# Attention and two GLU layers on one core: two small loads moved to ScalarE's queue, merged output stores, another accumulator bank

## The chip, the cores and the metric

The kernel runs on one core of one Trainium2 chip. The metric is the device time of one execution in microseconds (us); the time of a version is the median of its runs. One core has five engines that run side by side and wait for each other through semaphores: TensorE (PE; weight loads are PEld), VectorE (DVE), ScalarE (ACT), GpSimd (POOL) and SyncE (SP). Sixteen DMA engines move data between HBM and the on-chip memories. An engine starts a transfer by an issue instruction in its own queue; SP does nothing else.

## The reference

Inputs are q, k and v of shape (4 batches, 8 heads, 576 tokens, 64) in float32, a matrix omega (128 x 64) and six weight matrices. Per head, `phi(x) = exp(h - max h) / sqrt(m)` with `h = x_s omega^T - |x_s|^2 / 2`, where `x_s` is x scaled by 64^(-1/4). Then `kv = phi(k)^T v`, `z = sum of phi(k)`, and the result is `phi(q) kv / (phi(q) z + 1e-6)`. The heads are put side by side, giving 2304 rows of 512, and two GLU layers follow: `(silu(x Wg) * (x Wv)) Wo`, and the same with a sigmoid and other weights. The widths are 512, 1536 and 512. The output is 2304 x 512 in float32.

## The kernel before

**Attention.** It is worked off in 16 pairs of heads. A batch's 576 tokens are 512 main tokens and 64 last tokens. The main tokens of q and k are loaded by `Pair.load` (line 340) as 128 partitions of four tokens; the last tokens go to a tile `kqrem` of 128 partitions by 64 elements, where partition and row together stand for head and token. For the first pair alone (line 343) that is one transfer of 32 KB for k and one for q; their DRAM side is `src[0, :2, MAIN:, :]`, two stretches of memory of 64 rows each, one of either head. For other pairs a transfer per head is used (line 348). A list ORDER, written by hand, says which step of which pair stands after which in every engine's program. For the first pair ScalarE's order is: square of k (`mk`, line 379), square of the last tokens (`mr`, line 379), upper half of the transposed k (`hi_k`, line 406), square of q (`mq`). TensorE's order is: 14 idle transposes at the start, transposes of k (`tp_k`), of the last tokens (`tp_r`), products of k with omega (`pj`, line 420), transposes of q (`tp_q`), further products, and much later the products with v (`kv`, line 480). So `mr` and `tp_r` stand in front of everything else of the pair, and both read `kqrem`.

**Layers.** The 2304 rows are worked off in three sets of 768. The first layer of the first set runs beside the making of the weights; the other five passes (layer and set) use a Strassen form of the two first products, in which tiles X, Y, Z of PSUM (two banks each; X has two tiles in turn, Y and Z one each) take sums of products, and ScalarE and VectorE read them in `gate` and `total`. `gate` reads the first bank by an ACT instruction and the second by a DVE instruction (line 875) that stands a step later in the program. Behind each pass stands the third product: twelve slices, each with 18 matmuls into six accumulators, which are the two banks of Y, of Z and of one X tile (`acc`, line 981). In the three passes of the second layer the six accumulators b = 0..5 are copied to SBUF, by VectorE for even b and by ScalarE for odd b (lines 1007 to 1010), into four tiles used in turn (`u2`, `p5`, `s0`, `s2`, so b = 4 takes the tile of b = 0, and b = 5 that of b = 1). Each copy is stored to `out` from SP's queue by `store` (line 202); 128 main tokens of one batch take one transfer of 256 KB. In the very last pass (third set, `ahead is None`) the copies 2 and 5 are the last tokens of all four batches, 32 rows of each, and take four transfers of 64 KB, so SP issues twelve there.

Of the kernel before, what the change touches and what calls it, by code (L numbers as in the profile page):

```python
# [32 lines left out]
def tile_performer_attention__then__two_glu_layers(  # L33
# [25 lines left out]
    nc = tc.nc  # L59
    P = 128  # L60
    B, H, S, D = q.shape
# [3 lines left out]
    MAIN = NB * P  # L65
# [42 lines left out]
    class Weight:  # L108
# [11 lines left out]
        def load(self):  # L120
            l, c, n = self.key
            fs = slice(c * P, (c + 1) * P)
            w = weights[l][n]
            view = w[fs, :] if n == 2 else w[:, fs].rearrange("(k p) f -> p k f", p=P)
            if l == 0:
                self.res = wres.tile([P, KC * P], F32, tag=f"w{n}_{c}", name=f"w{n}_{c}")
                wf[self.key] = self.res
            if not self.cast:
                self.place()
                nc.sync.dma_start(  # L130
                    out=self.res if n == 2 else self.res.rearrange("p (k f) -> p k f", k=KC),
                    in_=view,
                )
                return
            raw64 = self.raw = wraw.tile([P, KC * P, 2], U32, name="raw64")
            nc.sync.dma_start(
                out=raw64.rearrange("p f w -> p (f w)")
                if n == 2
                else raw64.rearrange("p (k f) w -> p k (f w)", k=KC),
                in_=view.bitcast(U32),  # L140
            )
            self.lo, self.hi = raw64[:, :, 0], raw64[:, :, 1]
# [58 lines left out]
    def store(o, i):  # L201
        nc.sync.dma_start(out=o, in_=i)
# [69 lines left out]
    with ExitStack() as st:  # L272
# [47 lines left out]
        class Pair:  # L320
# [10 lines left out]
            def load(self):  # L331
                b, h0 = self.b, 2 * self.hp
                self.v = vbuf[self.n % len(vbuf)]
                if self.hp == 0:
                    rems[b] = spare(2 + b % 2, [P, NP, 2, D], name="kqrem"), vrbuf[b % len(vrbuf)]
                self.r, self.vr = [x[:, self.hp] for x in rems[b]]
                main = lambda x: x[b, h0:h0 + 2, :MAIN, :].rearrange("h (p i) d -> p h i d", i=NB)
                for n, name, src in (0, "k", k), (1, "q", q):
                    t = raw.tile([P, 2, NB, D], F32, name=name + "raw")
                    nc.sync.dma_start(out=t, in_=main(src))  # L340
                    setattr(self, name, t)
                    if self.n == 0:
                        nc.sync.dma_start(out=self.r[:, n, :], in_=src[0, :2, MAIN:, :])
                if self.n == 1 or self.hp == 0 and self.n > 0:
                    for n, src in (0, k), (1, q):
                        for h, hs in enumerate(halves):
                            tail = src[b, h::2, MAIN:, :].rearrange("n p d -> p n d")
                            nc.sync.dma_start(
                                out=rems[b][0][hs, self.hp:, n, :], in_=tail[:, self.hp:]
                            )  # L350
# [425 lines left out]
    with tc.manual_schedule():  # L776
# [3 lines left out]
        acc = [ps_a.tile([P, MAIN], F32, tag=f"acc{j}", name="acc") for j in range(6)]  # L780
        late = pool("late", 1, side="right")
        for c in range(FC):
# [11 lines left out]
            ahead = [of_w(0, c + 1, n) for n in range(2)] if c + 1 < FC and not w_next else []  # L794
            w2 = of_w(0, c, 2)
            assert {(0, c, 2)} | {(0, c + 1, n) for n in range(2) if ahead} <= done, c
            p, n = jobs[c]
# [16 lines left out]
            t = wsum.tile([P, 4, H2], F32, tag="s", name="wsums")  # L814
# [33 lines left out]
        ps_yz, ps_x = pool("ps_yz", 1, space=PSUM), pool("ps_x", 2, space=PSUM)  # L848
        tmp, hall = pool("tmp", 1), pool("hall", 1)
        bank = lambda p, tag: p.tile([P, 2, MAIN], F32, tag=tag, name=tag)  # L850
# [12 lines left out]
        rows = out.rearrange("(b s) e -> b s e", s=S)  # L863
# [69 lines left out]
        for at, (layer, n) in enumerate(STRASSEN):  # L933
            h, hs = {}, {}
            ahead = STRASSEN[at + 1][1] if at + 1 < len(STRASSEN) else None
            for p in range(FC // 2):
                X, Y, Z = bank(ps_x, "X"), bank(ps_yz, "Y"), bank(ps_yz, "Z")
                u2, p5 = [tmp.tile([P, 2, TS], F32, tag=x, name=x) for x in ("u2", "p5")]
                for c in (2 * p, 2 * p + 1):
                    h[c] = h_tile(c)  # L940
                h1, h2 = [[h[c][:, ab] for ab in range(2)] for c in (2 * p, 2 * p + 1)]
                for k in range(7):
                    dst = (X, Z, X, Y, X, Z, X)[k]
                    w = ready.pop(o)
                    for i in range(2):
                        for kk in range(2):
                            fs = slice(i * H2 + kk * P, i * H2 + (kk + 1) * P)
                            l, r = [u[:, fs] for u in w], xc[k, kk]
                            for j, (a, b) in enumerate(((0, 0), (0, 1), (1, 0))):
                                nc.tensor.matmul(  # L950
                                    dst[:, i, :TS],
                                    lhsT=l[a],
                                    rhs=r[b],
                                    start=k in (0, 1) and kk == 0 and j == 0,
                                    stop=kk == 1 and j == 2,
                                    skip_group_check=True,
                                )
                    if k == 0:
                        copy(both(Y), X)
                    if k == 1:  # L960
                        copy(p5, Z)
                    if k == 2:
                        copy(u2, X)
                    if k == 3:
                        after(1, partial(gate, layer, h1[0], both(Y)))
                    if k == 4:
                        total(layer, h2[1], X, p5)
                    if k == 5:
                        total(layer, h1[1], Z, u2)
                    if k == 6:  # L970
                        after(1, partial(gate, layer, h2[0], both(X)))
                    clock += 1
                    run()
                    prepare(o + AHEAD)
                    o += 1
                    for _ in range(1 + (k == 0)):
                        next(making, None)
                    if p == FC // 2 - 1 and k in (3, 5):
                        c = (k - 3) // 2
                        hs[c] = h_split(c)  # L980
            acc = [bank(ps_yz, "Y"), bank(ps_yz, "Z"), bank(ps_x, "X")]
            acc = [t[:, i, :] for t in acc for i in range(2)]
            for c in range(FC):
                w, now = ready.pop(o), hs.pop(c)
                if layer == 0:
                    second(acc, now, w, c == 0, c == FC - 1)
                else:
                    for b in range(6):
                        js = slice(b % 3 * P, (b % 3 + 1) * P)
                        l = [u[:, b // 3, js] for u in now]  # L990
                        three(acc[b], l, w, c == 0, c == FC - 1)
                clock += 2
                run()
                if c + 2 < FC:
                    hs[c + 2] = h_split(c + 2)
                prepare(o + AHEAD)
                o += 1
                for _ in range(2):
                    next(making, None)
                if ahead is not None:  # L1000
                    x_parts(ahead, c)
            for b in range(6):
                if layer == 0:
                    result(acc, n, LAST[b])
                    continue
                t = tmp.tile([P, DM], F32, tag=("u2", "p5", "s0", "s2")[b % 4], name="o")
                if b % 2:
                    nc.scalar.activation(t, acc[b], AF.Copy)
                else:
                    nc.vector.tensor_copy(t, acc[b])  # L1010
                q, ab = 3 * n + b % 3, b // 3
                batch = q // 2
                if batch < B:
                    i = 2 * (q % 2) + ab
                    dst = rows[batch, :MAIN, :].rearrange("(p i) e -> i p e", i=NB)[i]
                    store(dst, t)
                    continue
                for batch in range(B):
                    half = REM // 2
                    dst = rows[batch, MAIN + ab * half:MAIN + (ab + 1) * half, :]  # L1020
                    store(dst, t[batch * half:(batch + 1) * half])
        assert next(making, "none") == "none"


# [32 lines left out]
```

## Time and profile before

| what | value |
|---|---|
| median of 3 runs | 1054.29 us (1053.64 to 1056.53) |
| the profiled execution | 1055.49 us |
| its span, first to last instruction | 1053.7 us |
| PE busy | 1019.9 us, 97% of the span |
| DVE, ACT busy | 71%, 57% |
| DMA queue of SP | 49.5% of sixteen engines' span |

The profile shows one execution. Busy shares are means over stages with different limits: over the span the matmul engine is hardly ever idle, and its few idle stretches lie at the start and behind the last matmul, with some in the middle where weights are made. The granted clock of TensorE has two levels, 1.2 and 2.4 GHz, shown as 0.5 and 1.0. A timeline row gives start, duration, engine, line and tiles, and in brackets how long the engine had been idle and what released it. A row of the windows gives a stretch, its length, then for PE, PEld, DVE, ACT and POOL the busy time and in brackets the instructions that started, the granted clock, the share of the DMA engines and GB/s.

### The profile page before, as it was taken

The numbers are of one execution on the slowest core, as the hardware profiler recorded it, in microseconds if no ns is written. First come the engines' busy times: TensorE is split into PE (matmuls) and PEld (weight loads), VectorE is DVE, ScalarE is ACT, GpSimd is POOL, SyncE is SP. The second block draws the span as 40 slices with busy tenths as digits, with TensorE's granted clock in tenths as the row PEclk, the third lists the DMA queues.
The fourth block names the chain that finished last, engine by engine and source line by source line (L and its number), as shares of the span: only waits on it lengthen the run. The fifth ranks groups of instructions, "written<-read, shape, count | busy, mean of one in ns | idle before, by whom it ended". The sixth has DMA issues, their size and how long they took to land.

```text
span 1053.7 us, 17289 instructions
## 1 busy us (share of the span) xinstructions
PE 1019.9 (97%) x6079; PEld 956.8 (91%) x6079; DVE 752.0 (71%) x1526; ACT 595.7 (57%) x1259; POOL 86.4 (8%) x110
## 2 busy tenths in 40 slices
PE   8999999889999999999999999999999999999997
PEld 7999999889889989989899889898899998999985
DVE  6899996759785677887777886877655565556642
ACT  6999996324333655545555455655555554555532
POOL 2111112111110000000000000011000000000000
PEclk8999999999999999999999999999999999999999
DMA  7443422599794677756788666888244442444421
GB/s 204 137 127 111 107 81 81 157 238 258 215 263 142 172 221 225 213 163 179 199 239 251 172 178 197 259 245 214 81 150 131 130 114 67 141 130 125 117 79 61
DMA packets 138156, 173.15 MB, mean 164 GB/s; under 512 B 32852, under 2 KB 87124, under 8 KB 138068
## 3 DMA queue, kind: packets, MB, share of 16 engines
q1 hardware_dynamic: 129140, 155.78, 49.5%
q0 software_dynamic: 8928, 16.26, 8.6%
q8 instruction: 48, 0.79, 0.3%
q14 instruction: 40, 0.33, 0.1%
HBM read 122.72 MB, written 33.03 MB: 148 GB/s over the span
## 4 chain that ended last, share of the span: by engine, by line
PE 65%; DMA 11%; DVE 10%; issue 7%; ACT 4%; SPq 1%; POOL 0%; ACTq 0%; DVEq 0%; POOLq 0%
PE X L950 13%; PE Z L950 7%; DMA wp<-wf 6%; PE pj L420 4%; PE Y L950 4%; PE X L735 3%; PE Y L735 3%; PE kv L480 3%; PE Z L735 3%; ACT vh L238 3%; PE o L506 2%; DVE vl L242 2%; DMA raw<-in_moe_w_gate_dram 2%; PE acc L735 2%; DMA w<-mag 2%
## 5 line engine op out<-in xcount | busy, mean ns | idle before, releaser
L242 DVE TENSOR_TENSOR vl<-wp,vh 128x512 fp32r<-128x512 f32 x270 | 186.1, 689 | 147.6 <-ACT vh L238 147.3
L238 ACT ACTIVATE vh<-wp 128x512 fp32r<-128x512 f32 x270 | 167.5, 620 | 30.3 <-DMA wp<-wf 26.9
L950 PE MATMUL X<-xhi,vh 128*128 128x384 f32 x480 | 161.4, 336 | 5.6 <-DVE p L891 3.5
L950 PE MATMUL X<-xhi,vl 128*128 128x384 f32 x480 | 160.6, 335 | 0.1
L950 PE MATMUL X<-xlo,vh 128*128 128x384 f32 x480 | 160.4, 334 | 0.0
L882 ACT ACTIVATE hh<-h 128x768 fp32r<-128x768 f32 x60 | 50.6, 844 | 107.2 <-PE X L261 67.4
L883 DVE TENSOR_TENSOR hl<-h,hh 128x768 fp32r<-128x768 f32 x60 | 57.5, 958 | 64.9 <-ACT hh L882 64.7
L950 PEld LDWEIGHTS X<-xhi,vh 128*128 128x128 f32 x480 | 90.1, 188 | 8.9 <-issue 5.6
L950 PEld LDWEIGHTS X<-xhi,vl 128*128 128x128 f32 x480 | 90.1, 188 | 0.4 <-DVE vl L242 0.4
L950 PEld LDWEIGHTS X<-xlo,vh 128*128 128x128 f32 x480 | 90.1, 188 | 0.2
L950 PE MATMUL Z<-xhi,vh 128*128 128x384 f32 x240 | 81.4, 339 | 3.1 <-ACT vh L238 1.9
L950 PE MATMUL Z<-xhi,vl 128*128 128x384 f32 x240 | 81.5, 340 | 0.9
L950 PE MATMUL Z<-xlo,vh 128*128 128x384 f32 x240 | 80.3, 335 | 0.0
L151 ACT ACTIVATE mag<-raw 128x512 f32<-128x512 f32 x72 | 48.3, 673 | 38.5 <-DMA w<-mag 18.8
L260 PE MATMUL pg<-xhi,whi 128*128 128x384 f32 x160 | 56.1, 351 | 11.4 <-ACT s L806 11.4
L183 POOL DMA_DIRECT2D res<-mag x36 | 31.1, 864 | 385.2 <-DVE mag L177 370.1
L262 PE MATMUL pg<-xhi,wlo 128*128 128x384 f32 x160 | 55.5, 347 | 0.0
L261 PE MATMUL pg<-xlo,whi 128*128 128x384 f32 x160 | 55.5, 347 | 0.0
L950 PEld LDWEIGHTS Z<-xhi,vh 128*128 128x128 f32 x240 | 45.1, 188 | 6.0 <-ACT vh L238 4.2
L874 ACT ACTIVATE g<-p 128x384 f32<-128x384 f32 x30 | 15.8, 526 | 61.3 <-DVE p L891 61.3
L950 PEld LDWEIGHTS Z<-xhi,vl 128*128 128x128 f32 x240 | 45.0, 188 | 4.3 <-DVE vl L242 4.1
L177 DVE SCALAR_TENSOR_TENSOR mag<-raw,mag 128x512 f32<-128x512 uint32 x72 | 48.1, 687 | 0.8
(208 smaller groups left out, 2680.0 us busy)
## 6 DMA issues: line engine op xcount, KB each, us to landing
wp<-wf SPq DMA_DIRECT2D x210, 256.0 KB, 2.8
wp<-ws SPq DMA_DIRECT2D x60, 256.0 KB, 2.7
raw<-in_moe_w_gate_dram SPq DMA_DIRECT2D x24, 512.0 KB, 4.3
raw<-in_moe_w_val_dram SPq DMA_DIRECT2D x24, 512.0 KB, 4.4
raw<-in_moe_w_out_dram SPq DMA_DIRECT2D x24, 512.0 KB, 5.2
wf<-wsums SPq DMA_DIRECT2D x48, 256.0 KB, 4.8
res<-mag POOLq DMA_DIRECT2D x36, 256.0 KB, 5.2
w<-mag POOLq DMA_DIRECT2D x26, 256.0 KB, 8.6
```

The source lines that it names most:

```text
L151: nc.scalar.activation(self.mag, self.hi.bitcast(F32), AF.Abs, scale=REBIAS)
L177: nc.vector.scalar_tensor_tensor(self.mag, self.lo, 2.0**-52, self.mag, ALU.mult, ALU.mult)
L238: nc.scalar.activation(self.parts[0], self.src, AF.Copy)
L242: self.eng.tensor_tensor(lo, self.src, hi.bitcast(F32), ALU.subtract)
L260: nc.tensor.matmul(o, lhsT=l[0], rhs=r[0], start=start, stop=False)
L261: nc.tensor.matmul(o, lhsT=l[0], rhs=r[1], start=False, stop=False)
L262: nc.tensor.matmul(o, lhsT=l[1], rhs=r[0], start=False, stop=stop)
L420: nc.tensor.matmul(out_ap, lhsT=l[:, i, :], rhs=r, start=n == 0, stop=n == 2)
L735: nc.tensor.matmul(o, lhsT=l[a], rhs=r[b], start=start and i == 0 and not (tail and j % 2), stop=stop and i == 2, skip_group_check=tail,)
L882: nc.scalar.activation(hi, h[c], AF.Copy)
L883: nc.vector.tensor_tensor(lo, h[c], hi.bitcast(F32), ALU.subtract)
L950: nc.tensor.matmul(dst[:, i, :TS], lhsT=l[a], rhs=r[b], start=k in (0, 1) and kk == 0 and j == 0, stop=kk == 1 and j == 2, skip_group_chec ...
```

## The change

Three things are changed. The two loads of the first pair's last tokens are issued by ScalarE and not by SP. In the copies of the second layer's three passes ScalarE takes b = 0 and 1, VectorE takes 2 to 5; the last tokens of all four batches go out in one transfer of 256 KB instead of four, so six transfers are left at the end; in the very last pass the stores of b = 2 and b = 4 are issued by ScalarE. In the very last pass a second X tile is allocated, and the sixth accumulator is its first bank and no longer the second bank of the first X tile.

```diff
                     if self.n == 0:
-                        nc.sync.dma_start(out=self.r[:, n, :], in_=src[0, :2, MAIN:, :])
+                        nc.scalar.dma_start(out=self.r[:, n, :], in_=src[0, :2, MAIN:, :])
...
             acc = [bank(ps_yz, "Y"), bank(ps_yz, "Z"), bank(ps_x, "X")]
+            if ahead is None:
+                acc.append(bank(ps_x, "X"))
             acc = [t[:, i, :] for t in acc for i in range(2)]
+            if ahead is None:
+                acc[5:] = acc[6:7]
...
-                if b % 2:
+                if b // 2 == 0:
                     nc.scalar.activation(t, acc[b], AF.Copy)
                 else:
                     nc.vector.tensor_copy(t, acc[b])
                 q, ab = 3 * n + b % 3, b // 3
                 batch = q // 2
+                queue = nc.scalar if ahead is None and b in (2, 4) else nc.sync
                 if batch < B:
                     i = 2 * (q % 2) + ab
                     dst = rows[batch, :MAIN, :].rearrange("(p i) e -> i p e", i=NB)[i]
-                    store(dst, t)
-                    continue
-                for batch in range(B):
+                    queue.dma_start(out=dst, in_=t)
+                else:
                     half = REM // 2
-                    dst = rows[batch, MAIN + ab * half:MAIN + (ab + 1) * half, :]
-                    store(dst, t[batch * half:(batch + 1) * half])
+                    dst = rows[:, MAIN + ab * half:MAIN + (ab + 1) * half, :]
+                    queue.dma_start(out=dst, in_=t)
```

## Rows read from the trace of the kernel before

**Rows 1.** The page: busy time, share of the span, instructions.
```profile
PE 1019.9 (97%) x6079; PEld 956.8 (91%) x6079; DVE 752.0 (71%) x1526; ACT 595.7 (57%) x1259; POOL 86.4 (8%) x110
```
**Rows 2.** Chain of waits, 0 to 40 us: start, duration, what.
```profile
2.90 4.61 DMA kqrem<-in_q_dram
...
10.39 0.85 PE tp_q L400 x4
11.24 1.29 PE pj L420 x6
...
18.58 0.77 PE pj L420 x6
19.35 0.44 PE tp_q L400 x4
```
**Rows 3.** Timeline of ScalarE, 0 to 17 us.
```profile
0.75 1.28 ACT L379 ACT_TABLE_LOAD   x1 [0.75 <-PEq L1041]
...
7.81 0.58 ACT L406 ACTIVATE hi_k<-tp_k 128x512 fp32r<-128x512 f32 x1
```
**Rows 4.** Timeline of TensorE, the first 17 us.
```profile
4.86 0.60 PE L400 MATMUL tp_k<-ident,kraw 128*128 128x128 f32 x4
...
16.46 0.39 PE L480 MATMUL kv<-vr,fk 128*128 128x130 f32 x2
```
**Rows 5.** Windows of the start: busy time by engine, clock, DMA.
```profile
4.63:8.05 3.42, 1.13 (x8) 0.73 (x7) 1.29 (x4) 0.46 (x2) 0.86 (x3) 1.00 0.81 226
8.05:14.87 6.82, 6.42 (x27) 5.80 (x28) 4.43 (x13) 3.77 (x12) 1.42 (x2) 0.50 0.97 245
```
**Rows 6.** Timeline of the copies at the end, 1030 to 1054 us.
```profile
1044.14 0.69 DVE L1010 COPY o<-Y 128x512 f32<-128x512 f32 x1 [3.83 <-PE Y L262]
...
1045.50 0.69 DVE L1010 COPY o<-Z 128x512 f32<-128x512 f32 x1 [0.67 <-PE Z L262]
...
1047.11 0.69 DVE L1010 COPY o<-X 128x512 f32<-128x512 f32 x1 [0.92 <-DMA out_dram<-o]
1047.88 0.60 ACT L1008 ACTIVATE o<-X 128x512 f32<-128x512 f32 x1 [1.06 <-DVE o L1010]
```
**Rows 7.** Chain of waits, 1044 to 1054 us.
```profile
1044.86 2.13 DMA out_dram<-o
```
**Rows 8.** SP's last issue, and the landing of the last three issues.
```profile
1050.66 0.42 SPq L202 DMA_DIRECT2D out_dram<-o  x1
...
out_dram<-o SPq DMA_DIRECT2D x3, 64.0 KB, 2.0
```
**Rows 9.** Timeline of SP's queue, 0 to 8 us.
```profile
1.68 0.70 SPq L343 DMA_DIRECT2D kqrem<-in_k_dram  x1
...
2.90 0.57 SPq L343 DMA_DIRECT2D kqrem<-in_q_dram  x1
```
**Rows 10.** DMA issues, 0.7 to 0.8 and 10.1 to 10.2 us: KB, us to landing.
```profile
om<-in_omega_dram SPq DMA_DIRECT2D x1, 32.0 KB, 1.9
...
vr<-in_v_dram SPq DMA_DIRECT2D x1, 64.0 KB, 3.6
```
**Rows 11.** DMA packets from 3.55 to 4.00 us, then from 4.00 to 4.45.
```profile
DMA packets 104, 0.06 MB, mean 136 GB/s; under 512 B 58, under 2 KB 104, under 8 KB 104
...
DMA packets 103, 0.08 MB, mean 180 GB/s; under 512 B 32, under 2 KB 103, under 8 KB 103
```
**Rows 12.** Window of the last two passes.
```profile
800.00:1030.00 230.00, 230.00 (x1218) 215.96 (x1217) 132.60 (x200) 117.86 (x203) 0.00 (x0) 1.00 0.40 112
```
**Rows 13.** DMA from 1045.6 to 1047.2 us: packets, and the share of sixteen engines.
```profile
DMA packets 302, 0.56 MB, mean 347 GB/s; under 512 B 31, under 2 KB 31, under 8 KB 302
...
q1 hardware_dynamic: 302, 0.56, 95.2%
```
**Rows 14.** Timelines around the first slice of the last third product.
```profile
1001.10 0.39 PE L260 MATMUL X<-vh,hh 128*128 128x512 f32 x1
...
1001.82 0.55 DVE L875 TENSOR_TENSOR h<-g,X 128x384 f32<-128x384 f32 x1
```

## Prediction, before the result was known

> **What bounds the kernel now.** I read the page first: TensorE is busy for 97% of the span [rows 1], so over most of it only TensorE's own work counts, and I look for what the change moves at the two ends, where TensorE stands still. Next the chain of waits over the first 40 us: from 2.90 to 7.51 us it consists of one load, the second of the first pair's two small ones [rows 2]. ScalarE's square of the last tokens needs that load, and `hi_k`, from which all products of the pair follow, stands behind the square in program order: it starts at 7.81 [rows 3], although its own input, the transposed k, was ready at 5.46 [rows 4]. The windows show what this costs further on: the granted clock, 1.0 up to 8.05 us, is 0.5 from there to 14.87, behind a stretch in which TensorE was busy for 1.13 of 3.42 us [rows 5]. Last I read the end: the copies run one after the other, and VectorE and ScalarE take turns on the two banks of one PSUM tile; the chain goes through the store of the first copy, whose SBUF tile the fifth needs again [rows 6, 7]; SP's twelfth issue starts at 1050.66 and its data land about 2.0 us later [rows 8], at 1052.66, some 1.0 us ahead of the span's end.
>
> **The change part by part.**
>
> *The two small loads.* They leave SP's queue, where they took 0.70 + 0.57 us [rows 9], so every load behind them can be issued about 1.3 us sooner. On ScalarE they have cover: nothing but the load of the function table runs there until k has landed. If they are issued ahead of that table load, the second is issued near 1.5 us, else near 2.8 (0.75 + 1.28 + 0.70) [rows 3, 9]. How soon do they land? The omega load, just as large at 32 KB, needs 1.9 us when it is alone [rows 10]; the small load needed 4.61 [rows 2]. Two things make the difference: it stands behind 256 KB transfers in one queue, and it does not use all DMA engines. From 4.00 to 4.45 us, 32 packets of under 512 B (only the small loads have such) make 18 GB/s, about what one engine moves; from 3.55 to 4.00 us 58 make 33 GB/s, about two [rows 11]. So 32 KB take 1.0 us at that rate, two loads 2.0, and sharing the engines with k and q some more. Issued at 0.75 and 1.5 us, the second should land between 4.4 and 5.2 us; then ScalarE waits for it no longer, and `hi_k` starts when the transposes end, at 5.5 in place of 7.81: **-2.3 us**. Bounds: at best that (the transposes come late next); at worst, with the table load ahead and landing near 6.5, -0.9.
>
> *The clock.* Starting the products at 6.1 instead of 8.4 closes most of the idle stretch ahead of 8.05 us, so the clock may stay at its upper level. What half the clock costs: a group of six products takes 1.29 us at half and 0.77 at full clock, four transposes 0.85 and 0.44 [rows 2]. Up to ScalarE's next wait there are two such groups and one set of transposes: 2 x 0.52 + 0.41 = 1.45 us. Behind it ScalarE and VectorE are nearly as long as TensorE, and TensorE at full clock has new holes, in which the clock may fall later. Bounds -1.5 and +0.5; I take **-1.0**, nearer to the full price, since the cause of the fall goes. What is late next are v and its last tokens for `kv`, at 16.46 us [rows 4] less 3.3, that is 13.2; the last of these loads is issued at 10.12 and lands 3.6 us later [rows 10], 1.3 us sooner after the change: 12.4. That is a cover of 0.8 us.
>
> *The copies at the end.* ScalarE copies both banks of Y from 1044.14 on, 0.60 us each; VectorE both of Z from 1045.50 on, 0.69 each; so the turn-taking between engines goes. The fifth copy still waits for the first store: issue near 1044.76 plus 2.13 gives 1046.9, so it runs from 1047.0 to 1047.7, the sixth to 1048.4, as before (1048.48) [rows 6, 7]. No gain there. The stores on ScalarE stand behind its last copy and delay nothing. In the two passes before, the same turn-taking goes, and the next pass's tiles come free sooner; TensorE has no idle time there to give back (230.00 of 230 us busy [rows 12]): 0, either way.
>
> *The merged stores.* Six SP issues fewer: the last store starts at 1048.4 in place of 1050.66. With all sixteen engines it would land 2.13 us later, at 1050.6: -2.0 us, the lower bound. But the merged store has the form of the small load: one side 128 partitions, the other a few separate stretches of memory, here four. Two stretches kept about two engines busy, so I expect four here.
> The Trainium skill ("DMA: Bandwidth & Descriptors", section "Why a DMA increments its semaphore by 16 and not by 1") says that a transfer is spread over the largest number of engines, up to 16, which divides the slowest dimension of both its sides; for the small load that is 2 and for the merged store 4. By that rule the sum comes out as I take it, by its absence as in the first rival; the rates above agree with 2.
> An engine moves 347 / 0.952 / 16 = 22.8 GB/s with packets of 2 KB [rows 13]. Each of the four has to move 64 KB of b = 2, 64 KB of b = 5 and 16 KB each of b = 3 and 4, that is 164 kB, or 7.2 us. Work begins with the store issued at 1046.2; 256 KB at 347 GB/s are 0.75 of the 2.13 us, so 1.4 is what a transfer needs besides. 1046.2 + 1.4 + 7.2 = 1054.8 against 1052.66: +2.1 us. If the two merged stores went to different engines, b = 5 alone would land at 1048.4 + 1.4 + 2.9 = 1052.7: 0.0. I take **+2.1**: that the small load needed 2.7 us more than omega while its data need 1.0 says that it queues behind others on its own engines.
>
> *The sixth accumulator.* Its copy no longer shares a tile with the fifth; both stand on VectorE, so nothing comes of it. It costs where it is allocated: the second X tile is still being read when the first slice wants it. VectorE reads it from 1001.82 to 1002.37; the slice's sixth group would start at 1001.10 [rows 14]. That read is the other bank and later in the program, so I take **0**; if the whole tile has to be free, TensorE waits 1.3 us. Below zero nothing is to be had, as TensorE has no gap there [rows 12].
>
> **Sum.** -2.3 - 1.0 + 2.1 + 0 = -1.2 us; the profiled execution's 1055.49 becomes 1054.3. That execution lies 1.2 above the median of the runs shown, so for the median 1054.29 I expect 1053.1 us. What this kernel's measurements can tell from no change is about 0.3%, 3.2 us, so this is no visible change. The likeliest case's own range is 1050.3 (a whole clock gain, no queueing: -2.3 - 1.5 + 0) to 1056.5 (-0.9 + 2.1 + 1.3, less or more).
>
> **Rivals.**
>
> *The merged store uses all engines.* For it: every other store of the end does, at 347 GB/s. Against it: the small load, of the same form, does not. Tail -2.0, head -3.3: 1054.29 - 5.3 = 1049.0 us, faster.
>
> *The loads gain only their issue time.* The engines, and not the queue, hold the load: k and q still share its two engines. For it: in 4.00 to 4.45 us the small packets get one engine's rate while larger ones flow. Against it: the wait of 2.7 us is mostly its place in the queue. Then the second load is issued at 1.5 instead of 2.90: -1.4, the clock falls as before, and the end costs +2.1: 1055.0 us, slower than before, though not visibly; with the table load ahead -0.1 and 1056.3. It decides where the second load lands later than 7.5 - 2.1 = 5.4 us.
> The Trainium skill states this ("DMA: Bandwidth & Descriptors", section "Issuing engines are not separate DMA queues"): transfers issued from several engines run on the same sixteen DMA engines and interleave, and issuing from several saves issue time alone.
>
> *The merged store uses fewer than four engines.* With two, each has 2 x 128 + 2 x 16 = 288 KB, 295 kB or 12.9 us of work, and the last data land at 1060.5: +7.8, in sum +4.5, 1058.8 us, slower. It outweighs the head as soon as an engine's work passes 8.4 us. For it only that I know no store of this form in the trace; against it that two stretches had two engines.
>
> **How the numbers follow.** Forecast 0.53, all engines 0.20, issue time alone 0.20, fewer than four 0.07. Faster by over 0.3% (under 1051.1 us): nearly all of the first rival, 0.18, and the forecast's lower end, 0.12: 0.30. Slower by over 0.3% (above 1057.5): 0.06 of the third rival and 0.01 of the second: 0.07. Within: 0.63. The range is 1048.6 to 1056.0: it takes in most of the first rival and of the second, and leaves out the third and the outer ends.
>
> **What would show it.** In the changed kernel's chain of waits the small load is gone from the first 8 us, `hi_k` starts near 5.5 us, and the window from 8.05 us on shows a clock of 1.0 for most of its length. At the end there are six stores, the last issued near 1048.4 less the head's gain, and the two merged ones take over 4 us to land, the last one longest, with DMA rates near 90 GB/s. TensorE has no idle time at the first slice of the last third product. I am wrong if the merged store lands within 2.5 us (then 1049), if `hi_k` still waits for the small load, or if the head's gain is lost before the layers begin.

## The result and the profile after

The changed kernel takes 1061.73 us in the median of 6 runs (1059.77 to 1063.78), the kernel before 1053.97 (6 runs): a ratio of 1.0068, interval 1.0048 to 1.0088. It is slower by about 7.2 us (5.1 to 9.3). The forecast was 1053.1 us and no visible change, with a range up to 1056.0.

The page of the changed kernel, its first two lines: the span grew by 8.3 us, from 1053.7 to 1062.0, TensorE's busy time by 3.5, from 1019.9 to 1023.4 [rows 1].

```profile
span 1062.0 us, 17296 instructions
...
PE 1023.4 (96%) x6079; PEld 958.3 (90%) x6079; DVE 753.7 (71%) x1529; ACT 594.4 (56%) x1256; POOL 86.9 (8%) x110
```

**The start.** The chain of waits of the changed kernel, 0 to 40 us (start, duration, what): the small load is still what everything waits for, and it takes 5.30 us where it took 4.61 [rows 2]. Six products still take 1.29 us.

```profile
0.75 1.16 ACTq L343
...
1.94 5.30 DMA kqrem<-in_q_dram
...
10.13 0.85 PE tp_q L400 x4
10.98 1.29 PE pj L420 x6
...
18.32 0.77 PE pj L420 x6
```

ScalarE's timeline in the changed kernel: both loads are issued ahead of the table load, as the forecast hoped, and still `hi_k` starts at 7.55 and not at 5.5 [rows 3].

```profile
2.51 1.28 ACT L379 ACT_TABLE_LOAD   x1 [2.51 <-issue]
...
7.33 0.31 ACT L379 ACTIVATE mr<-kqrem 128x128 f32<-128x128 f32 x1 [2.25 <-DMA kqrem<-in_q_dram]
7.55 0.58 ACT L406 ACTIVATE hi_k<-tp_k 128x512 fp32r<-128x512 f32 x1
```

**The last third product.** TensorE's and VectorE's timelines of the changed kernel in its first slice, then the window of the last two passes: one wait of 1.24 us, released by VectorE's read of the old X tile, and 228.76 us of work where there were 230.00 [rows 12, 14]. Matmuls overlap, so the idle time is less than the delay: from the start of the matmul ahead of the wait to that of the thirteenth behind it the kernel before needs 2.94 us (1000.88 to 1003.82), the changed one 4.45 (1002.37 to 1006.82), which is 1.5 us more.

```profile
1003.31 0.55 DVE L875 TENSOR_TENSOR h<-g,X 128x384 f32<-128x384 f32 x1
```
```profile
1004.00 0.47 PE L260 MATMUL X<-vh,hh 128*128 128x512 f32 x1 [1.24 <-DVE h L875]
```
```profile
800.00:1030.00 230.00, 228.76 (x1214) 214.89 (x1213) 132.91 (x200) 116.52 (x202) 0.00 (x0) 1.00 0.40 113
```

**The end.** The timeline of the changed kernel from 1045.5 us on: the copies keep their order, as worked out, and the last of six stores is issued at 1051.40, 1.6 us behind the last matmul (1049.43 + 0.39).

```profile
1047.14 1.09 ACT L1012 ACTIVATE o<-Y 128x512 f32<-128x512 f32 x2 [4.82 <-PE Y L262]
...
1048.50 1.29 DVE L1014 COPY o<-Z 128x512 f32<-128x512 f32 x2 [5.19 <-PE Z L262]
...
1049.22 0.64 ACTq L1025 DMA_DIRECT2D out_dram<-o  x1
1049.43 0.39 PE L262 MATMUL X<-vh,hl 128*128 128x512 f32 x1
1050.02 1.35 DVE L1014 COPY o<-X 128x512 f32<-128x512 f32 x2 [0.23 <-DMA out_dram<-o]
1050.74 0.35 ACTq L1021 DMA_DIRECT2D out_dram<-o  x1
1051.40 0.69 SPq L1025 DMA_DIRECT2D out_dram<-o  x1
```

DMA of the changed kernel from 1047 to 1061 us, in 40 slices of 0.35 us (share of the sixteen engines in tenths, and GB/s): full rate of up to 392 GB/s for the first two stores, then a stretch in which several stores share the engines, then a plateau at two to three tenths, some 80 GB/s, that runs out at 1059.9. In the kernel before the engines moved 347 GB/s in the mean with its stores [rows 13].

```profile
DMA  0000399950578696665332222222222221100000
GB/s 0 0 0 0 140 386 375 392 205 0 123 228 222 222 334 176 140 152 111 64 88 76 88 64 64 70 76 82 99 88 82 82 94 53 59 29 29 0 0 0
```

From the last matmul to the end of the span the kernel before needs 6.9 us, the changed one 12.2. So of the profiles' 8.3 us, 5.3 lie behind the last matmul, 1.5 are the wait, and the start gives 0.3 back; the other 1.8 lie in the middle, where of the change there are only the copies of the two earlier passes of the second layer (see what stays open).

### The profile page after: what moved, and what is told of

It is laid out like the page before. It is cut to its first block, busy times and chain, and to the rows that moved or that the text cites. A ratio compares the mean times of both kernels' runs of the same rounds, so it can differ in the third digit from the quotient of the medians.

```text
span 1062.0 us, 17296 instructions
## 1 busy us (share of the span) xinstructions
PE 1023.4 (96%) x6079; PEld 958.3 (90%) x6079; DVE 753.7 (71%) x1529; ACT 594.4 (56%) x1256; POOL 86.9 (8%) x110
## 4 chain that ended last, share of the span: by engine, by line
PE 68%; DVE 10%; DMA 10%; issue 6%; ACT 4%; POOL 0%; SPq 0%; ACTq 0%; DVEq 0%; POOLq 0%
PE X L950 14%; PE Z L950 7%; DMA wp<-wf 5%; PE Y L950 4%; PE pj L420 4%; DMA raw<-in_moe_w_gate_dram 3%; PE X L735 3%; PE Y L735 3%; PE kv L480 3%; PE Z L735 3%; PE o L506 2%; PE acc L735 2%; DVE vl L242 2%; ACT vh L238 2%; PE pg L260 2%
```

## The experiments

Each kernel was profiled, and those with an interval were timed against the kernel before on the same chip. "The end" is the span less the end of the last matmul, from one execution of each; the kernels of the table ran on several chips, so ratios are compared and not times:

```
kernel            span    last matmul ends   the end   ratio to before (interval)
before            1053.7   1046.83             6.9     -
changed           1062.0   1049.82            12.2     1.0068 (1.0048 to 1.0088)
merged_only       1057.0   1045.55            11.5     1.0047 (1.0032 to 1.0062)
acc_only          1052.8   1045.92             6.9     1.0029 (1.0013 to 1.0044)
head_only         1052.1   1045.25             6.9     1.0016 (1.0003 to 1.0030)
copies_only       1052.4   1045.64             6.8     1.0007 (0.9995 to 1.0019)
spread_only       1050.1   1044.54             5.6     0.9979 (0.9963 to 0.9996)
spread_all        1054.6   1048.97             5.6     1.0018 (1.0000 to 1.0035)
head_four         1054.8   1047.98             6.8     0.9991 (0.9971 to 1.0011)
best_mix          1048.9   1043.45             5.5     0.9988 (0.9968 to 1.0007)
merge_last        1056.9   1047.30             9.6     -
merge_first       1055.7   1047.63             8.1     -
after_one_queue   1059.9   1048.39            11.5     -
spread_head       1050.1   1044.64             5.5     0.9984 (0.9969 to 0.9999)
```

**merged_only.** Only the merged stores.

```diff
-                for batch in range(B):
-                    half = REM // 2
-                    dst = rows[batch, MAIN + ab * half:MAIN + (ab + 1) * half, :]
-                    store(dst, t[batch * half:(batch + 1) * half])
+                half = REM // 2
+                dst = rows[:, MAIN + ab * half:MAIN + (ab + 1) * half, :]
+                store(dst, t)
```

> The kernel before with one part of the change: the last tokens' outputs (copies 2 and 5) go out in one transfer of 256 KB each, both from SP; copies, loads and accumulators as before. Theory E (a transfer whose DRAM side is four stretches runs on four DMA engines): each of the four has 64 + 16 + 16 + 64 KB, which is 7.2 us at the 22.8 GB/s of an engine before, begun near 1047.1, so the last store lands near 1054.7 and not 1052.7, at a rate of some 90 GB/s: slower by 2 to 3 us. Theory Q (the 5.3 us that the end is longer come from issuing on two queues, not from the form of the store): the merged stores land some 2 us after their issue and the kernel is 2 us faster, since SP has six issues fewer.

Measured: ratio 1.0047, 5.0 us; the end is 11.5 us. Theory Q falls: one queue, and the end is 4.6 us longer. DMA of merged_only from 1050.5 to 1053.5 us: a quarter of the engines is busy (25.5% of 16 is 4.1), at 85 GB/s.

```profile
DMA packets 132, 0.25 MB, mean 85 GB/s; under 512 B 8, under 2 KB 8, under 8 KB 132
...
q1 hardware_dynamic: 132, 0.25, 25.5%
```

So theory E is right on the engines and too small on the cost: 4.6 us measured, 2 to 3 expected. The stores on all engines that stand between the two merged ones land 5.4 and 5.1 us behind their issue; in the kernel before the first of these two needed 2.2.

**acc_only.** Only the second X tile for the sixth accumulator.

```diff
+            if ahead is None:
+                acc.append(bank(ps_x, "X"))
             acc = [t[:, i, :] for t in acc for i in range(2)]
+            if ahead is None:
+                acc[5:] = acc[6:7]
```

> The kernel before with one part of the change: in the very last pass the sixth accumulator lies in a second X tile. Theory W (the new tile waits until VectorE has read the old one): TensorE stands still once for some 1.2 us in the first slice of the last third product, as in the changed kernel, and nothing behind it gives that back: slower by 1.2 us. Rival: the copies of the fifth and sixth accumulator, by VectorE and ScalarE, no longer wait for each other, and the end gains up to 0.7 us of it: slower by 0.5.

Measured: ratio 1.0029 (1.4 to 4.6 us slower); the end is 6.9 us as before. The wait is there by itself, in VectorE's and TensorE's timelines of acc_only:

```profile
999.38 0.55 DVE L875 TENSOR_TENSOR h<-g,X 128x384 f32<-128x384 f32 x1
```
```profile
1000.07 0.47 PE L260 MATMUL X<-vh,hh 128*128 128x512 f32 x1 [1.25 <-DVE h L875]
```

Theory W holds: 1.25 us of idle time, 1.5 by the starts of the matmuls around it, and the end gives nothing back. What the timing says beyond 1.5 is not explained by this trace.

**head_only.** Only the two loads from ScalarE.

```diff
-                        nc.sync.dma_start(out=self.r[:, n, :], in_=src[0, :2, MAIN:, :])
+                        nc.scalar.dma_start(out=self.r[:, n, :], in_=src[0, :2, MAIN:, :])
```

> The kernel before with one part of the change: the two loads of the first pair's last tokens are issued by ScalarE. Theory S (the loads share their DMA engines with the large loads, whatever queue they come from): the square of the last tokens starts 0.3 us sooner, products run as slowly as before up to 14 us, and the time is 0.3 us shorter, which timing can't tell from nothing. Theory M (the 2 us that the changed kernel loses between 170 and 440 us come from the shifted loads): slower by 1.5 to 2 us.

Measured: ratio 1.0016 (0.3 to 3.2 us slower). Chain of waits of head_only, first 12 us; behind it the same stretch of merged_only, whose start is that of the kernel before:

```profile
0.75 1.14 ACTq L343
...
1.92 5.53 DMA kqrem<-in_q_dram
```
```profile
2.90 3.79 DMA kqrem<-in_q_dram
```

Issued 1.0 us sooner, the load lands at 7.45; in merged_only, from SP, at 6.69; before at 7.51 [rows 2]. The shift of the queue gains nothing that stands out from what the same start does in different executions. Neither theory is settled. The trace doesn't show theory M's loss, for its last matmul ends at 1045.25, ahead of that of before; but the timing, 1.7 us slower, is what theory M forecast, and the 0.3 us gain of theory S lies outside its interval.

**copies_only.** Copies by other engines, two stores from ScalarE, the last tokens in four transfers each.

```diff
-                if b % 2:
+                if b // 2 == 0:
                     nc.scalar.activation(t, acc[b], AF.Copy)
...
+                queue = nc.scalar if ahead is None and b in (2, 4) else nc.sync
...
-                    store(dst, t[batch * half:(batch + 1) * half])
+                    queue.dma_start(out=dst, in_=t[batch * half:(batch + 1) * half])
```

> The kernel before with one part of the change: ScalarE copies accumulators 1 and 2, VectorE the other four, and in the very last pass ScalarE issues the stores of the third and fifth copy; the last tokens still go out in four transfers of 64 KB each. If the copies' turn-taking cost something: the fourth copy's store is no longer behind four issues on SP, the sixth copy ends near 1048.4 as before, its four issues take 1.7 us from there, and the last data land some 0.8 us sooner than before: faster by 0.8 us. Rival (two queues slow each other down where both have stores): the same or slower by up to 1 us.

Measured: ratio 1.0007, within what can be told from nothing; the end is 6.8 us. The expected 0.8 us are not there; a loss of up to 2 us isn't excluded.

**spread_only.** Merged stores with another order of the last tokens.

```diff
-        return view[:, :, 2 * P + b * REM // 2:2 * P + (b + 1) * REM // 2]
+        return view[:, :, 2 * P + b:3 * P:B]
...
+                half = REM // 2
+                dst = rows[:, MAIN + ab * half:MAIN + (ab + 1) * half, :]
+                store(dst.rearrange("b s e -> s b e"), t)
```

> The kernel before with merged stores in another form: the last tokens stand in the order token, batch in the tile (their columns are written with a stride of four), so that the store's DRAM side begins with 32 tokens of four batches each and no longer with four stretches; still two transfers of 256 KB in place of eight of 64 KB, all from SP. Theory E (the four stretches put the store on four DMA engines): now all engines take part, the last store lands 2.1 us after an issue near 1.7 us behind the last matmul, and the time from the last matmul to the end is near 5 us, against 6.9 before and 11.5 with four stretches: 2 us faster than before. Rival (a store over all batches is slow in itself, for its rows lie apart in memory): the end stays near 11 us.

Measured: ratio 0.9979 (0.4 to 3.9 us faster); the end is 5.6 us. The same bytes in the same two transfers now move at full rate, in the DMA of spread_only from 1046 to 1047 us, and the six stores land 2.3 us after issue in the median (issues from 1042 to 1050 us):

```profile
DMA packets 202, 0.38 MB, mean 377 GB/s; under 512 B 18, under 2 KB 18, under 8 KB 202
...
q1 hardware_dynamic: 202, 0.38, 101.0%
```
```profile
out_dram<-o SPq DMA_DIRECT2D x6, 256.0 KB, 2.3
```

Theory E holds, its rival falls: what made the merged store slow is the order of its dimensions, not that it reaches over all batches.

**spread_all.** The changed kernel with that order (the two edits of spread_only on top of it, with the store's queue kept).

```diff
-                    dst = rows[:, MAIN + ab * half:MAIN + (ab + 1) * half, :]
-                    queue.dma_start(out=dst, in_=t)
+                dst = rows[:, MAIN + ab * half:MAIN + (ab + 1) * half, :]
+                queue.dma_start(out=dst.rearrange("b s e -> s b e"), in_=t)
```

> The changed kernel, all of its parts, with the last tokens in the order token, batch, as in spread_only. Theory E: the end shrinks from 12.2 to about 5 us; the wait for the second X tile (1.2 us) stays; about 0.5 us faster than before, which timing hardly tells from nothing, and 6 to 7 us faster than the changed kernel. Rival (issuing on two queues is what made the end long): the end stays above 9 us.

Measured: ratio 1.0018 (0 to 3.7 us slower) in place of 1.0068; the end is 5.6 us in place of 12.2. By ratio this one edit takes away 5.3 of the changed kernel's 7.2 us; by trace the end is 6.6 us shorter. The wait for the X tile and the middle stay; so 0.5 us faster than before, as expected of it, it is not.

**head_four.** The small loads in one transfer per head.

```diff
-                        nc.sync.dma_start(out=self.r[:, n, :], in_=src[0, :2, MAIN:, :])
+                        for h, hs in enumerate(halves):
+                            nc.scalar.dma_start(out=self.r[hs, n, :], in_=src[0, h, MAIN:, :])
```

> The kernel before, with the first pair's last tokens loaded by ScalarE in four transfers of 64 rows, one per head and input, in place of two whose DRAM side is two stretches. Theory F (the small loads are late since each runs on two DMA engines, which they share with the large ones): over all engines they land by 5 us, the square of the last tokens no longer waits, the first products start near 6 us in place of 8.4, and the kernel is 2 us faster. Rival (any load issued beside the large ones lands late): they land near 7 us as before and nothing is gained.

Measured: ratio 0.9991 (0.9971 to 1.0011), unclear. ScalarE's timeline of head_four: the loads are landed at 6.3 us, not by 5 and not near 7; `hi_k` starts 1.2 us sooner than before.

```profile
0.75 1.20 ACTq L344 DMA_DIRECT2D kqrem<-in_k_dram  x2
1.98 1.26 ACTq L344 DMA_DIRECT2D kqrem<-in_q_dram  x2
...
6.37 0.31 ACT L380 ACTIVATE mr<-kqrem 128x128 f32<-128x128 f32 x1 [1.17 <-DMA kqrem<-in_q_dram]
6.59 0.58 ACT L407 ACTIVATE hi_k<-tp_k 128x512 fp32r<-128x512 f32 x1
```

Between the two theories, and the other traces bear it out: `hi_k` starts at 6.44 to 6.59 us in the three kernels with one transfer per head (head_four, best_mix, spread_head), at 7.15 to 7.78 in the four with two stretches from ScalarE (changed, head_only, spread_all, after_one_queue), and at 6.96 to 7.81 in the seven with two stretches from SP. So the spread form lands sooner, and the queue makes no difference that these traces show. The timing can't tell the gain.

**best_mix.** head_four, copies_only and the merged stores of spread_only together (their edits as shown).

> Made of the parts: the four small loads from ScalarE, copies by ScalarE (first two) and VectorE (the rest), the third and fifth copy stored by ScalarE, merged stores with tokens ahead of batches, accumulators as before. Theories E and F together: 2 us at the start and 2 us at the end, 4 us or 0.4% faster than before. If the start gains nothing, 2 us; if neither, the same as before.

Measured: ratio 0.9988 (0.9968 to 1.0007), not the 0.4% that were expected. The trace has both gains (the end is 5.5 us); the timing doesn't settle it.

**merge_last, merge_first.** One of the two last-token copies merged, the other in four transfers (`b == 2` in place of `b == 5` for merge_first).

```diff
+                if b == 5:
+                    store(rows[:, MAIN + ab * half:MAIN + (ab + 1) * half, :], t)
+                    continue
```

> The kernel before, where of the two last-token copies only the sixth goes out in one transfer, the third still in four. From the last matmul to the end the kernel before needs 6.9 us, merged_only 11.5. Theory E1 (4.6 us are mostly the queue: the last store's engines still have the third copy's 64 KB each and the next two stores' 16 KB to do): alone, the last store's 64 KB per engine take 2.9 us behind 1.4 of overhead, it is issued 1.7 us behind the last matmul, and the end is about 7.5 us. Theory E2 (a store on four engines has some 3 us of cost of its own besides): the end is 10 us or more.

Measured: the end is 9.6 us, between the two. DMA of merge_last from 1051 to 1055 us, when its one merged store is at work:

```profile
DMA  1231840008500200211231312222322232223211
GB/s 82 61 61 41 61 20 0 0 0 41 20 0 0 20 0 20 61 61 41 61 82 61 61 41 102 102 82 82 143 102 82 82 143 102 82 82 143 102 61 61
...
q1 hardware_dynamic: 118, 0.24, 23.8%
```

In the first 1.5 of the 4.0 us the engines move 0 to 82 GB/s, with gaps, 27 in the mean; the plateau, 97 GB/s in the mean from 1053.5 us on, comes later. At the 22.8 GB/s of an engine before, 91 for four, the same bytes would have taken 0.45 us, so the slow beginning costs about 1.1 of the 2.1 us by which E1 fell short (9.6 against 7.5). Another 0.8 is the issue: SP starts it at 1049.82, 2.5 us behind the last matmul and not 1.7.

> The kernel before, where only the third copy goes out in one transfer, the sixth still in four of 64 KB. Theory E1 (queueing on the same four engines): the four last stores have a share on those engines and wait there behind 64 KB of the third copy, so the end is still longer than with four transfers each, near 7.5 to 9 us, though the last store itself is spread over all engines. Rival (the third copy's store is long done when the last ones come): the end is 6 us or less, since SP has three issues fewer.

Measured: the end is 8.1 us, 1.2 longer than before, though the four last stores run on all engines and three issues are saved. Theory E1's time is met, its mechanism in part. The stores of the fourth and fifth copy land 5.3 and 5.1 us behind their issue, where the fourth needed 2.2 before, so they do wait behind the merged store. But the last store lands 1.9 us behind its issue, close to the 1.7 of before; it is the issue that is late, 5.1 us behind the last matmul where it was 3.8 [rows 8], since SP spends 1.50 and 1.33 us on two of the four last issues, which took 0.33 to 0.43 us each before. SP's queue in merge_first, from 1049.3, 1050.9 and 1052.8 us:

```profile
1049.32 1.50 SPq L202 DMA_DIRECT2D out_dram<-o  x1
...
1050.87 1.33 SPq L202 DMA_DIRECT2D out_dram<-o  x1
...
1052.71 0.43 SPq L202 DMA_DIRECT2D out_dram<-o  x1
```

The two alone cost 2.7 and 1.2 us at the end, both together 4.6.

**after_one_queue.** The changed kernel with every store issued by SP.

```diff
-                queue = nc.scalar if ahead is None and b in (2, 4) else nc.sync
+                queue = nc.sync
```

> The changed kernel with all stores issued by SP and none by ScalarE. If issuing from two queues adds to the end (12.2 us in the changed kernel, 11.5 in merged_only): the end is 11.5 or less. If the queue makes no difference: 12.2 as in the changed kernel. In both cases TensorE waits 1.2 us for the second X tile.

Measured: the end is 11.5 us, as in merged_only, against 12.2. The second queue adds 0.7 us here, seen once.

**spread_head.** head_four's loads and spread_only's stores; copies and accumulators as before.

> A version meant to beat both: the kernel before, with the first pair's last tokens loaded by ScalarE in four transfers, and merged stores in the order token, batch; copies, queues of the stores and accumulators as before. From the traces of head_four and spread_only: start 1.6 us sooner, end 1.3 us shorter, so 2.9 us or 0.3% faster than before. Rival (what the start gains is lost where the weights are made): 0.1% faster.

Measured: ratio 0.9984 (0.1 to 3.3 us faster than before, about 1.7). The expected 2.9 us and the rival's 0.1% both lie inside. Both this kernel and spread_only beat the kernel before and the changed one; their intervals overlap, so the loads of head_four are not shown to add anything.

## Why the prediction was wrong

*The two small loads, -2.3 us: wrong, nothing that can be told from none.* The forecast took the load's wait to be mostly its place in SP's queue, so that a queue of its own would let it pass. The table load did stand behind the loads, which was the good case, yet the second load landed at 7.24 us in place of the forecast 4.4 to 5.2. It was issued at 1.94 and not at 1.5, since the first issue took 1.16 us, and it then needed 5.30 us. The trace of the kernel before, at 7.51, is the latest of seven with the loads on SP, so the 0.3 us against it are no gain. What I had read from the packets, that these loads run on about two engines, is the likely reason: if those two engines also have their share of every 256 KB load, a queue of its own gives the small packets turns there, not an engine. head_only shows no gain; head_four, with the load in a form that uses more engines, lands near 6.3. The second rival (issue time alone, 1055.0) had this mechanism; even its 1.4 us were not there. The Trainium skill ("DMA: Bandwidth & Descriptors", section "Issuing engines are not separate DMA queues") says that transfers of several issuing engines interleave on the same DMA engines, and only issue time is saved. The trace agrees on the first and shows no time saved: the loads behind were not issued 1.3 us sooner. The four small loads of line 348 held SP for 4.42 us (2.19 + 2.23) in place of 2.70 (1.44 + 1.26), and its second load of v's last tokens is issued at 10.54, before at 10.12. SP's queue in the kernel before, then in the changed one:

```profile
4.67 1.44 SPq L348 DMA_DIRECT2D kqrem<-in_k_dram  x2
6.16 1.26 SPq L348 DMA_DIRECT2D kqrem<-in_q_dram  x2
```
```profile
3.39 2.19 SPq L348 DMA_DIRECT2D kqrem<-in_k_dram  x2
5.62 2.23 SPq L348 DMA_DIRECT2D kqrem<-in_q_dram  x2
```

*The clock, -1.0: wrong, nothing in this execution.* Six products took 1.29 us and four transposes 0.85, as before. The windows are no help here: the column of the granted clock (third from the end, ahead of DMA share and GB/s) reads 1.00 for the changed kernel's 8.05 to 14.87 us, and the durations contradict it.

```profile
4.63:8.05 3.42, 1.94 (x8) 1.27 (x7) 1.30 (x4) 1.17 (x4) 0.87 (x3) 1.00 0.61 171
8.05:14.87 6.82, 6.68 (x30) 5.85 (x30) 4.47 (x14) 3.79 (x13) 1.42 (x2) 1.00 0.89 225
```

The forecast misread the same column: "1.0 up to 8.05 us" [rows 5] doesn't hold for the kernel before either. Its 14 idle transposes, from 1.81 on, took 3.10 us, 0.22 each, which is the pace of four in 0.85; only the four transposes of k at 4.86 (0.60 us in all) ran at the upper level, and in the changed kernel they took 1.06. So the clock had hardly been up, and the idle stretch ahead of 8.05 us is not shown to be the cause of its fall. The price was right: spread_all, whose start is that of the changed kernel, ran these products at the upper level and needed 6.5 us from the first of them to the first `kv` product (7.78 to 14.29), the changed kernel 8.0 (8.18 to 16.20). In head_four the products began at 7.22 and the granted clock still was 0.50 from 8.5 to 11.3. No run shows what decides it.

*The copies: right.* The sixth copy ends 1.6 us behind the last matmul, before 1.7; copies_only shows no change.

*The merged stores, +2.1: right in kind, mis-sized, +5.3.* Four engines it is: 85 GB/s and 25.5% of sixteen in merged_only, where rates near 90 were forecast, and the stores do queue on the same four, as the sum had it. By the forecast the last one lands 8.0 us behind the last matmul (1054.8 - 1046.83), and the span ends 1.0 later. In merged_only data flowed until 9.5 us behind it (1055.0 - 1045.55), in the changed kernel until 10.1 (1059.9 - 1049.82), and the span ended 2.0 and 2.1 us behind the last data. So in merged_only 1.5 us were missing in the flow of data and 1.0 behind it. Of the flow, a part is the slow beginning (merge_last shows it alone; in merged_only the engines move 66 GB/s in the mean from 1046.4 to 1047.4 us, before the next stores join), and a part the ending: from 1054.3 to 1055.3 us 23 GB/s are moved, one engine's rate. The forecast's overhead of 1.4 us, taken from a store on all engines, held neither. The second queue adds 0.7, seen once. The forecast's count of bytes by rate gave the plateau and no more. The Trainium skill's rule for the number of engines ("DMA: Bandwidth & Descriptors", section "Why a DMA increments its semaphore by 16 and not by 1") agrees with both forms: largest common divisor (up to 16) 4 for four stretches, 25.5% measured; 16 with 32 tokens first, 101.0% measured.

*The sixth accumulator, 0: wrong, +1.5.* The bound's upper end (1.3) came true and a little more, 1.24 us of idle time and 1.5 of delay: the new tile waits for the last read of the old one, though that read is in the other bank and later in the program.

*The sum.* -0.3 + 0 + 5.3 + 1.5 = 6.5 us, inside the measured 5.1 to 9.3. All four wrong steps were wrong in the same direction; the merged stores and the accumulator are what made the kernel slower. The bounds of the likeliest case were added up wrongly, too: from 1054.29 its terms give 1050.5 and 1056.8, not 1050.3 and 1056.5, which changes nothing here. The first rival (all engines) is what spread_only does; the third (fewer than four) has the sign and 4.5 of the size, for a reason that is not the true one.

*What stays open.* The middle of the kernel, from the attention to the last pass, differs between executions by more than most effects here: the last matmul ends anywhere from 1043.45 to 1049.82 us in the kernels of the table, also where their middles are the same, and 29 runs of the kernel before took 1050.34 to 1057.09. The traces say where. Up to VectorE's last `xr` (line 543), at 176.06 us in the kernel before, each trace keeps the lead that it has at its first `kv` product, to 0.1 us: 0.3 us in the changed kernel, 1.6 in head_four. From there to VectorE's last read of X (1001.82 us before [rows 14]) traces gain up to 1.8 us on that of before (acc_only) or lose up to 2.8 (head_four); the changed kernel lost 1.8. As merge_last, which is the kernel before up to its last copies, loses 1.9 there, no trace shows that the change causes it, and none shows what does. It wasn't tried to give the sixth accumulator a second tile without the wait.

## What to carry to other kernels

Before you merge transfers, look at the outermost dimension of both sides: here a store whose outer dimension is 4 moved at a quarter of the rate (85 against 377 GB/s) and held up what came behind, while the same bytes with 32 outermost went at full rate. Moving a late load to another queue did not help here; another form of the load did. The tile that was taken over early waited for the last reader of its predecessor, in the other bank; look for that reader before you allocate. And one trace is one execution: with the same instructions the small load landed at 6.66 to 7.51 us, so a gain of 0.3 us read from two traces says nothing.

## What the runs showed of the hardware

A store of 256 KB on four engines can cost more than four times the transfer time of one on sixteen: in merge_last 0.24 of its 0.26 MB took 4.0 us, where 256 KB at 347 GB/s are 0.75 us and four times that 3.0, with a beginning at 0 to 82 GB/s before the plateau. The end grew by 2.7 us for one such store. Stores that use all engines are held up behind it: 5.1 to 5.4 us to land in place of 2.2 (merged_only, merge_first). So is the engine that issues: behind such a store two of SP's issues took 1.50 and 1.33 us in place of 0.33 to 0.43 (merge_first), and with the small loads on ScalarE four issues at the start took 4.42 in place of 2.70. And the start of a kernel is not the same in each execution: with the same instructions there, the small load landed at 7.51 us in the kernel before and at 6.69 in merged_only, and the same products took 6.5 us in one execution and 8.0 in another (spread_all, changed kernel).
